# Loading the convolution's rows on GpSimd's queue, and a third landing buffer for the second weights

## The chip, the cores and the metric

The kernel runs on one core of a Trainium2 chip. The core has a matrix engine (TensorE, PE in the profile), three engines for elementwise work (VectorE is DVE, ScalarE is ACT, GpSimd is POOL) and SyncE (SP), which here only issues DMA transfers. PE's weight loads are shown apart as PEld. Every engine works through its own instructions in order; semaphores hold an instruction back until what it needs is there. A transfer is issued by an instruction on some engine's queue and moved by 16 DMA engines that all queues share.

The metric is the time of one execution in microseconds (us) on the device. The kernel before takes 1116.93 us, the median of three runs (1115.04 to 1117.27).

## What is computed

The input is one sequence of 2048 rows of 576 numbers. Its layer norm goes two ways, and both results are added to the input:

```
xn  = layernorm(x)
out = x + S4(xn) + silu(xn @ w1) @ w2          # w1: 576 x 4608, w2: 4608 x 576
S4:  A = A_re + i A_im,  dt = exp(log_dt)       # 576 channels, 128 states
     K[d,l] = Re sum_n C[d,n] dt[d] B[d,n] exp(dt[d] A[d,n] l)
     y[:,d] = causal convolution of xn[:,d] with K[d,:]  + xn[:,d] * Dskip[d]
```

The convolution is done by transforms: the kernel K and xn are brought to a spectrum, multiplied, and brought back.

## The kernel before, in words

**The feed-forward part** fills most of PE's time. The 2048 rows are taken in two halves, each half in two blocks of 512 rows, and the 4608 hidden columns in nine chunks of four tiles of 128 (t = 0 to 3). For a block and a chunk, `up` (lines 331 to 352) multiplies by the first weights into a PSUM tile `ph`, applies SiLU on ACT (`gf`), and splits the result into a high and a low part (`gh`, `gl`); `down` (354 to 376) multiplies by the second weights into `po` for four groups of 128 rows and two halves of 288 columns, and DVE adds that to the accumulators `acc`. Each product is made of three matmuls: high by high, high by low, low by high.

**Weights.** Each weight tile is loaded into a landing buffer and then split. For the second weights, `load_w2` (310 to 316) issues one transfer of 128 x 576 numbers into a buffer `w2r`, and `split_w2` (318 to 329) has ACT cast it to `w2h` (line 324) and DVE subtract to get `w2l` (326). A buffer is free again when its `w2l` is made. The buffers lie in the pool `wp`; for t = 2 and 3 of the very first chunk they lie in `pa`, and of the very last chunk in `yp`. All weight loads but the first are issued on SP's queue. The loads for a chunk are written into the steps of the chunk before it: t = 0 and 1 after the first block's second `up`, t = 2 in the second block's first step, t = 3 in its fifth. The loads for the last chunk are written earlier, all at the start of the last chunk but one.

**The spectral part** (`spectral`, from line 749) runs beside the second half of the feed-forward part. For 16 groups it loads spectra on POOL's queue, makes small matmuls (line 795), multiplies on DVE, goes back through matmuls into `pb` (line 846), and stores two tiles `yo` to DRAM (`d<-yo`, line 851). Its tiles lie in a pool `kl`.

**The tail** (`tail`, lines 894 to 914) begins when `kl` is released, because the pool `yp` takes that memory. It loads the stored accumulators of the first half (`r0`, line 900; the profile writes `r`), and the convolution's rows: `conv_load` (926 to 933) issues for one j two transfers of 64 x 4 x 288 numbers into a tile `ys`, of which there are eight. `add_conv` (935 to 954) makes sixteen small matmuls `py` for a pair of j, adds them with DVE (line 952), and calls `conv_load` for two further j. Finished rows are stored (line 194) on the queues of POOL, SP and ACT.

**Order.** The program text gives each piece of work a place, and side work is woven into the feed-forward steps by due times (`weave`, `side`). The order that each engine gets is then made by a planner, which runs the program on a modelled timeline (`schedule_with_timeline_sim=True`, line 1132) and puts each engine's ready instructions in the order of that timeline. A change of a queue or of a buffer count can therefore move instructions on every engine. The program gives the transfers of SP and ACT eight counters in turn and those of POOL eight others; an issue waits until the transfer that used its counter before has landed.

Of the kernel before, what the change touches and what calls it, by code (L numbers as in the profile page):

```python
# [11 lines left out]
F32 = mybir.dt.float32  # L12
# [7 lines left out]
P = 128  # L20
L = 2048
D = 576
# [21 lines left out]
def kernel(  # L44
# [22 lines left out]
    nc = tc.nc  # L67
# [38 lines left out]
    wp = ctx.enter_context(tc.tile_pool(name="wp", bufs=2))  # L106
# [160 lines left out]
    def ffn():  # L267
# [42 lines left out]
        def load_w2(half, c, t):  # L310

            first = half == 0 and c == 0
            last = half == 1 and c == NCH - 1
            r2 = (pa if first and t > 1 else yp if last and t > 1 else wp).tile([P, D], F32, tag="w2r", name="w2r", bufs=2)
            pins["load"] = nc.sync.dma_start(r2, w2v[:, c * FT + t, :]).ins  # L315
            R2[half, c, t] = r2

# [87 lines left out]
        for t in range(FT):  # L405
            load_w2(0, 0, t)
# [12 lines left out]
        for i, blk in enumerate(blocks):  # L419
# [4 lines left out]
            if half == 0 and c == NCH - 1:  # L424
                next_xt(b)

            after = {
                (0, "u0"): [(load_w1, 0)],
                (0, "u1"): [(split_w1, 0), (load_w2, 0), (load_w2, 1)],
                (0, "u2"): [(load_w1, 2)],  # L430
                (1, "u0"): [(split_w1, 2), (split_w2, 0), (load_w2, 2)],
                (1, "d3"): [(split_w2, 1), (load_w2, 3), (split_w2, 2)],
                (1, "u2"): [(split_w2, 3)],
# [460 lines left out]
    def tail():  # L894

        r0s = {}

        def load_r0(j):
            r0s[j] = yp.tile([P, 2, D], F32, tag="r0", name="r0", bufs=4)
            nc.sync.dma_start(r0s[j], dr0[j * P:(j + 2) * P, :].rearrange("(i p) d -> p i d", p=P))  # L900

        yield tail_at[0]
        with behind(pins["load"]):
            for j in (0, None, 2, None, None, None, None, None):
                conv_load()
                if j is not None:
                    load_r0(j)
        for j in range(0, 8, 2):
            if j == 2:
                load_r0(4)  # L910
                load_r0(6)
            yield tail_at[1 + j // 4] + j // 2 % 2 * tail_at[3]
            add_conv(j, (r0s[j][:, 0, :], r0s[j][:, 1, :]))
            store(r0s[j], j, (nc.gpsimd,))

    yss = {}
# [9 lines left out]
    def conv_load():  # L926

        j = next(order, None)
        if j is not None:
            yss[j] = yp.tile([P, 4, HD], F32, tag="ys", name="ys", bufs=8)  # L930
            for h in range(2):
                nc.sync.dma_start(yss[j][64 * h:64 * h + 64],  # L932
                                  d2[j * 256:(j + 1) * 256, h * HD:(h + 1) * HD].rearrange("(q r) d -> r q d", q=4))

    def add_conv(j, dsts):

        py = [pool.tile([P, 512], F32, tag=t, name="py") for pool, t in ((pss, "pss"),) * 3 + ((ps3, "ps3"),)]
        first = pins["pe"]
        for n in range(16):
            i, q1, q2, h = 1 - n // 8, n // 4 % 2, n // 2 % 2, 1 - n % 2  # L940
            o = 64 * q1 + 32 * q2
            rows = slice(64 * h, 64 * h + 64)
            with tc.high_priority() if n else nullcontext(), behind(first):
                mm = nc.tensor.matmul(py[2 * i + h][o:o + 32, :HD], s4[rows], yss[j + i][rows, 2 * q2 + q1],  # L944
                                      start=True, stop=True, tile_position=(64 * h, o), skip_group_check=True)
            if n == 0:
                first = mm.ins
        for i in range(2):
            del yss[j + i]
            for h in range(2):  # L950
                hs = slice(h * HD, (h + 1) * HD)
                nc.vector.tensor_add(dsts[i][:, hs], py[2 * i + h][:, :HD], dsts[i][:, hs])
        for _ in range(2):
            conv_load()
# [181 lines left out]
```

## Time and profile before

| | us |
|---|---|
| median of the runs | 1116.93 |
| the profiled execution | 1118.75 |
| its span, first to last instruction | 1116.9 |
| PE busy in the span | 1097.8 |
| PE waiting for `w2h` | 10.1 |
| landing time of a `w2r` load, median | 4.1 |
| landing time of a `ys` load, median | 7.1 |

The clock that PE was granted is 0.996 of full speed over the span. In a list of waits, a line names the engine and the work that waited, what it waited for, the total in us, how many times, and the longest. In a chain or a timeline, a line begins with its start and its duration in us. SPq is SP's queue issuing. In a transfer view, q1 is the queue of transfers that SP and ACT issue and q0 that of POOL, each with packets, MB and its share of the time of 16 DMA engines; an issue line ends with KB of one transfer and the median us from issue to landing.

### The profile page before, as it was taken

Reading aid. Unit: us, or ns where it says so; the run is one execution under the profiler, and the core shown is the slowest. Engines: PE = TensorE matmul, PEld = TensorE weight load, DVE = VectorE, ACT = ScalarE, POOL = GpSimd, SP = SyncE. Lnnn points to the kernel's source line nnn. Section 1 sums busy time; section 2 is a strip of 40 time slices with the busy share of each in tenths; the row PEclk is TensorE's granted clock in tenths of the full one; section 3 lists DMA queues with packets and bytes.
Section 4 is the critical chain, followed back from the end, with each engine's and each line's share of the span. In section 5 each row is a group of like instructions: output and inputs, shape, how many; then the busy total and the mean of one; then the engine's idle time right before and its main releaser. Section 6 shows DMA issues by size and latency. Waiting matters only on the chain. (4 is left out here: it accounts for less than half of the span.)

```text
span 1116.9 us, 23956 instructions
## 1 busy us (share of the span) xinstructions
PE 1097.8 (98%) x9807; PEld 962.2 (86%) x9807; DVE 892.1 (80%) x1431; ACT 660.7 (59%) x1030; POOL 141.8 (13%) x257
## 2 busy tenths in 40 slices
PE   9999999999999999999999999999999999996998
PEld 7989998899989888989999987878888888896886
DVE  7799899999999999999999637867786867442443
ACT  4665466676777676667777437576767576431220
POOL 1100000000000000011000033332332321000111
PEclk9999999999999999999999999999999999998999
DMA  9746512525252434275734185554555644294363
GB/s 254 203 122 166 148 45 60 129 72 130 72 130 72 109 99 93 73 185 178 187 108 97 42 215 164 172 158 143 178 178 159 191 136 121 82 239 127 92 164 86
DMA packets 174397, 150.22 MB, mean 135 GB/s; under 512 B 112544, under 2 KB 144048, under 8 KB 174160
## 3 DMA queue, kind: packets, MB, share of 16 engines
q1 hardware_dynamic: 156544, 93.77, 32.9%
q0 software_dynamic: 16992, 54.07, 15.4%
q8 instruction: 77, 1.26, 0.5%
q10 hardware_dynamic: 752, 0.85, 0.3%
q14 instruction: 32, 0.26, 0.1%
HBM read 104.13 MB, written 44.61 MB: 133 GB/s over the span
## 5 line engine op out<-in xcount | busy, mean ns | idle before, releaser
L367 PE MATMUL po<-w2h,gh 128*128 128x288 f32 x1152 | 338.6, 298 | 10.2 <-ACT w2h L324 10.1
L367 PE MATMUL po<-w2l,gh 128*128 128x288 f32 x1152 | 339.4, 296 | 0.4 <-DVE w2l L326 0.4
L367 PE MATMUL po<-w2h,gl 128*128 128x288 f32 x1152 | 337.0, 295 | 0.8 <-DVE gl L352 0.8
L367 PEld LDWEIGHTS po<-w2h,gh 128*128 128x128 f32 x1152 | 215.4, 188 | 26.9 <-ACT w2h L324 11.5
L367 PEld LDWEIGHTS po<-w2l,gh 128*128 128x128 f32 x1152 | 216.5, 188 | 7.8 <-issue 1.4
L367 PEld LDWEIGHTS po<-w2h,gl 128*128 128x128 f32 x1152 | 215.8, 188 | 3.3 <-issue 1.4
L349 ACT ACTIVATE gf<-ph 128x512 f32<-128x512 f32 (+1 forms) x146 | 85.7, 588 | 155.7 <-PE ph L343 145.8
L371 DVE TENSOR_TENSOR acc<-po,acc 128x288 f32<-128x288 f32 x288 | 125.9, 451 | 51.0 <-PE po L367 49.7
L341 PE MATMUL ph<-xh,w1h 128*128 128x512 f32 (+1 forms) x584 | 162.1, 390 | 0.0
L341 PE MATMUL ph<-xh,w1l 128*128 128x512 f32 (+1 forms) x584 | 159.7, 387 | 0.0
L341 PE MATMUL ph<-xl,w1h 128*128 128x512 f32 (+1 forms) x584 | 158.7, 387 | 0.0
L352 DVE TENSOR_TENSOR gl<-gf,gh 128x512 fp32r<-128x512 f32 (+1 forms) x148 | 98.6, 671 | 74.1 <-ACT gh L350 73.2
L341 PEld LDWEIGHTS ph<-xl,w1h 128*128 128x128 f32 x584 | 107.1, 188 | 21.5 <-issue 0.9
L341 PEld LDWEIGHTS ph<-xh,w1l 128*128 128x128 f32 x584 | 106.9, 188 | 21.0 <-issue 0.9
L341 PEld LDWEIGHTS ph<-xh,w1h 128*128 128x128 f32 x584 | 104.2, 188 | 18.1 <-issue 1.4
L350 ACT CAST gh<-gf 128x512 fp32r<-128x512 f32 (+1 forms) x148 | 89.3, 608 | 23.5 <-PE po L367 20.7
L174 POOL DMA_DIRECT2D d1u<-u x32 | 17.4, 545 | 463.5 <-ACT u L173 463.5
L326 DVE TENSOR_TENSOR w2l<-w2r,w2h 128x576 fp32r<-128x576 f32 x72 | 53.2, 750 | 18.7 <-ACT w2h L324 18.5
L324 ACT CAST w2h<-w2r 128x576 fp32r<-128x576 f32 x72 | 47.0, 672 | 31.6 <-DMA w2r<-in_B_w_dram 24.4
L663 ACT ACTIVATE c<-th,magic 128x1040 f32<-128x1040 f32 x36 | 42.1, 1168 | 37.1 <-DVE C L686 27.5
L832 ACT CAST yh<-y 128x576 fp32r<-128x576 f32 x32 | 21.6, 674 | 65.1 <-DVE y L829 53.2
L665 ACT ACTIVATE c<-th 128x1040 f32<-128x1040 f32 x36 | 38.7, 1075 | 32.8 <-DVE th L664 32.8
(196 smaller groups left out, 1779.4 us busy)
## 6 DMA issues: line engine op xcount, KB each, us to landing
w2r<-in_B_w_dram SPq DMA_DIRECT2D x72, 288.0 KB, 4.1
w1r<-in_B_w_dram SPq DMA_DIRECT2D x35, 512.0 KB, 4.0
d1u<-u POOLq DMA_DIRECT2D x32, 288.0 KB, 2.7
d1k<-stage SPq DMA_DIRECT2D x36, 256.0 KB, 4.7
u<-d1u POOLq DMA_DIRECT2D x16, 576.0 KB, 4.7
d<-yo POOLq DMA_DIRECT2D x32, 288.0 KB, 3.0
ys<-d SPq DMA_DIRECT2D x32, 288.0 KB, 7.1
xr<-dxn SPq DMA_DIRECT2D x16, 288.0 KB, 2.9
```

The lines of the kernel that those rows point to most:

```text
L174: nc.gpsimd.dma_start(d1u.rearrange("(p m j) d -> m j p d", m=2, j=NJ)[m, j], u1)
L324: pins["w2h"] = nc.scalar.copy(h2, r2).ins
L326: pins["w2l"] = nc.vector.tensor_sub(l2, r2, h2).ins
L341: nc.tensor.matmul(ph, w[:, kt, :], v[:, kt, a:e], start=n + kt == 0, stop=False)
L349: nc.scalar.activation(gf, ph, AF.Silu)
L350: pins["gh"] = nc.scalar.copy(gh, gf).ins
L352: pins["gl"] = nc.vector.tensor_sub(gl, gf, gh).ins
L367: pins["pe"] = nc.tensor.matmul(po[:, :HD], G[blk, t][g][:, js], W2[half, c, t][w][:, hs], start=n == 0, stop=n == 3 * FT - 1).ins
L371: nc.vector.tensor_add(acc[j][:, hs], po[:, :HD], acc[j][:, hs])
L663: nc.scalar.activation(c65, th, AF.Identity, bias=magic)
L665: nc.scalar.activation(c65, th, AF.Abs)
L832: nc.scalar.copy(yh, y)
```

## The change

Two lines change. In `load_w2` the landing buffer `w2r` has three instances instead of two where it lies in `wp`, which is everywhere but for t = 2 and 3 of the first and the last chunk. In `conv_load` the two transfers of a `ys` tile are issued on GpSimd's queue instead of SP's.

```diff
@@ load_w2
-            r2 = (pa if first and t > 1 else yp if last and t > 1 else wp).tile([P, D], F32, tag="w2r", name="w2r", bufs=2)
+            r2 = (pa if first and t > 1 else yp if last and t > 1 else wp).tile([P, D], F32, tag="w2r", name="w2r", bufs=2 if t > 1 and (first or last) else 3)
             pins["load"] = nc.sync.dma_start(r2, w2v[:, c * FT + t, :]).ins
             R2[half, c, t] = r2
@@ conv_load
             yss[j] = yp.tile([P, 4, HD], F32, tag="ys", name="ys", bufs=8)
             for h in range(2):
-                nc.sync.dma_start(yss[j][64 * h:64 * h + 64],
+                nc.gpsimd.dma_start(yss[j][64 * h:64 * h + 64],
                                   d2[j * 256:(j + 1) * 256, h * HD:(h + 1) * HD].rearrange("(q r) d -> r q d", q=4))
```

## The prediction

> **What bounds the kernel now.** I read the page's first part, then PE's waits, then the chain that ended last, and then SP's queue and the transfers where that chain stands still.
>
> ```profile
> span 1116.9 us, 23956 instructions
> PE 1097.8 (98%) x9807; PEld 962.2 (86%) x9807; DVE 892.1 (80%) x1431; ACT 660.7 (59%) x1030; POOL 141.8 (13%) x257
> ...
> PE po L367 <- ACT w2h L324: 10.1, 4, 8.6
> PE py L944 <- DVE r L952: 0.6, 1, 0.6
> PE po L367 <- DVE w2l L326: 0.4, 1, 0.4
> ```
>
> PE is busy for 98% of the span. The matmuls are the same in number and shape after the change, so only PE's idle time can be won: 1116.9 - 1097.8 = 19.1 us, part of it start and end. More than half of what can be won is one wait: of 10.1 us that PE waited for the high part of the second weights (w2h), 8.6 us are a single one. The chain shows where.
>
> ```profile
> 973.19 2.73 DMA d<-yo
> ...
> 978.45 7.02 DMA w2r<-in_B_w_dram
> ...
> 985.53 12.29 DMA w2r<-in_B_w_dram
> ...
> 998.45 10.58 DMA ys<-d
> ...
> 1009.10 9.89 DMA w2r<-in_B_w_dram
> ...
> 1019.01 0.68 ACT w2h L324
> 1019.68 0.04 issue
> 1019.73 1.09 PE po L367 x3
> ...
> 1025.21 2.72 PE ph L341 x12
> 1027.93 7.96 PE po L367 x60
> ```
>
> The last store of the spectral stage (d<-yo) lands at 975.92. From there the chain is transfers only, and PE comes back at 1019.73, when a tile of second weights that was issued at 1009.10 has landed (9.89 us) and been cast (0.68 us). It is the fourth tile (t=3) of the last chunk but one. SP's queue and the transfers show why it was so late:
>
> ```profile
> 976.19 0.38 SPq L288 DMA_DIRECT2D w1r<-in_B_w_dram  x1
> ...
> 977.82 1.06 SPq L315 DMA_DIRECT2D w2r<-in_B_w_dram  x2
> 978.92 2.55 SPq L932 DMA_DIRECT2D ys<-d  x2
> ...
> 984.17 0.54 SPq L288 DMA_DIRECT2D w1r<-in_B_w_dram  x1
> 985.53 0.35 SPq L315 DMA_DIRECT2D w2r<-in_B_w_dram  x1
> ...
> 992.72 13.40 SPq L932 DMA_DIRECT2D ys<-d  x10
> 1006.63 1.58 SPq L900 DMA_DIRECT2D r<-dr  x2
> 1009.10 11.73 SPq L315 DMA_DIRECT2D w2r<-in_B_w_dram  x3
> ...
> DMA packets 7330, 9.60 MB, mean 253 GB/s; under 512 B 480, under 2 KB 5741, under 8 KB 7328
> q1 hardware_dynamic: 7328, 9.57, 106.1%
> ys<-d SPq DMA_DIRECT2D x16, 288.0 KB, 10.4
> r<-dr SPq DMA_DIRECT2D x4, 576.0 KB, 10.2
> w2r<-in_B_w_dram SPq DMA_DIRECT2D x5, 288.0 KB, 9.4
> w1r<-in_B_w_dram SPq DMA_DIRECT2D x1, 512.0 KB, 11.7
> w1r<-in_B_w_dram SPq DMA_DIRECT2D x2, 64.0 KB, 11.0
> ```
>
> The last seven lines are the transfer view of 978 to 1016 us. All 16 DMA engines are full there (106.1% by this count) at 253 GB/s, all on SP's queue. The tile that PE waits for stands behind sixteen convolution loads of 288 KB, ten of which alone take 13.40 us to issue, because the built program lets an issue on SP wait for the transfer eight places before it.
>
> **The change, part by part.** *SP's queue loses 32 issues* (16 pairs). Of its work before the tile, 16 x 288 KB = 4.72 MB go. At 253 GB/s this is 18.7 us of transfer, twice the wait.
>
> *The third buffer.* Outside the first and last chunk a tile of second weights now waits for the split of the third tile before it, no longer of the second. In the built order t=2 stands right behind t=0 and t=1, and t=3 waits for the split of t=0 where it waited for that of t=1. The three smaller waits for w2h (10.1 - 8.6 = 1.5 us) and the one for its low part (0.4 us) are such late tiles, so I count 1.9 us gained. What stands behind these issues on SP goes out earlier with them.
>
> *POOL's queue gains 32 issues.*
>
> ```profile
> 971.34 0.30 PE L846 MATMUL pb<-yh,mm 128*128 128x288 f32 x1
> 972.65 1.08 POOL L851 DMA_DIRECT2D d<-yo  x2 [7.23 <-ACT yo L816]
> ...
> POOL out_dram L194 <- DVE r L952: 88.5, 4, 70.3
> ```
>
> At 1.08/2 = 0.54 us each that is 17.3 us of issuing, on a queue that idles up to 70.3 us after d<-yo: nothing on the path. In the built order twenty loads stand ahead of POOL's first output store; that store moves, the last ones do not, and the end is set by PE and the stores that follow it.
>
> *The planner orders every engine anew,* and this is where the change can lose what it gains. I counted in the two built orders, from the last matmul of the spectral stage (L846) to the first that needs the late tile. Before: 139 po and 92 ph. After: 111 po and 56 ph. With 7.96/60 = 0.133 and 2.72/12 = 0.227 us each that is 39.3 us before (971.34 + 39.3 = 1010.6, where PE did stop) and 27.4 us after: the spectral stage ends later in PE's order, and the tile is wanted sooner.
>
> SP cannot begin the load before the spectral stage's memory is free. That was 976.19 - 971.34 = 4.85 us after its last matmul, with nothing in that stretch that the change touches. In the new order SP then issues: w1r (640 KB), two w2r, all four r (576 KB each), 576 KB of the next w1r, and the tile. That is 640 + 576 + 2304 + 576 + 288 = 4384 KB = 4.49 MB that must land within 27.4 + 0.3 (PE drains what it has begun) - 4.85 - 0.72 (cast) = 22.1 us. About 1.5 us of it are latency: 288 KB alone took 2.73 us (d<-yo), 1.2 of them at 253 GB/s. There remain 20.6 us, so no wait needs 4.49/20.6 = 218 GB/s on SP's queue, while POOL's queue holds up to eight convolution loads at any time. How two full queues share the engines is the unknown. Two stretches of the spectral stage (656.5 to 661.5 and 680.5 to 683 us) have both queues full:
>
> ```profile
> DMA packets 1036, 1.51 MB, mean 301 GB/s; under 512 B 153, under 2 KB 786, under 8 KB 1035
> q1 hardware_dynamic: 820, 0.94, 66.7%
> q0 software_dynamic: 215, 0.56, 40.1%
> ...
> q1 hardware_dynamic: 255, 0.53, 71.1%
> q0 software_dynamic: 94, 0.22, 26.1%
> ```
>
> SP's queue (q1) got 0.94/5 = 188 and 0.53/2.5 = 212 GB/s, POOL's (q0) 112 and 88. The ends for the new wait: SP alone at 253 GB/s needs 17.7 us, no wait; half of 253 GB/s needs 35.6 us, a wait of 15.0 us. I take the two measured rates: 212 for the 3.24 MB of w2r and r (rows of 2304 bytes, as in the second stretch) and 188 for the 1.25 MB of w1r, 15.3 + 6.6 = 21.9 us, a wait of 1.3 us.
>
> The Trainium skill (DMA: Bandwidth & Descriptors, section Issuing engines are not separate DMA queues) says that transfers run on the same 16 engines whoever issues them, and that issuing from several engines saves only issue time. By this rule the 4.72 MB cost as much as before, and the move alone wins nothing; the two stretches agree that the queues share, and what I count on is the order in which bytes are served.
>
> *Other new waits of the new order* no row shows. Below they can be negative (the 0.6 us before py may go), above I allow 3 us, six of the mean small wait of 1.5/3 = 0.5 us. I take 1.0, two of them.
>
> **Sum.** The profiled execution took 1118.75 us (span 1116.9). -8.6 + 1.3 (the tile) - 1.9 (small waits) + 1.0 (new order) = -8.2, so 1110.5 in such an execution. The median of the runs, 1116.93, stands 1.82 below it: 1108.7.
>
> **The rivals.** *Even halves (slower).* If the engines give POOL's queue half their bytes, the tile lands 15.0 us late and the sum is -8.6 + 15.0 - 0.9 = +5.5: 1122.4. The point from which this decides is 4.49/(20.6 + 8.6 + 0.9) = 149 GB/s on SP's queue. Against it stand 188 and 212; for it, that neither stretch had the queues full for more than 5 us.
>
> *Turn by turn (no change).* If each queue sends one row in turn, SP's 2624 rows (1216 of 1024 bytes, 1408 of 2304) bring as many of 1152 from POOL, 3.02 MB: 7.51/0.253 = 29.7 us, a wait of 9.1 us, sum -0.4: 1116.5. Against it: 820 packets to 215 and 255 to 94, both stretches with q0 waiting.
>
> The Trainium skill (the same page, section Queues, rings and completion order) has each engine go round the queues it has work for, packet by packet, which would be this rival if a packet were one row. The counts do not agree with that reading.
>
> *Half the gain.* SP's queue reaches some 165 to 185 GB/s, or SP waits for its transfer eight places back while r is in flight: a wait of 3.7 to 6.6 us, 1111 to 1114.
>
> *The new order loses elsewhere (slower).* DVE at 80% is the next busiest; were its work put so that PE waits over 9 us in total, the time would pass 1117, up to 1120. Today PE waits 0.4 and 0.6 us for DVE in the rows above.
>
> *The convolution loads come too late from POOL.* After SP's bytes have landed at POOL's 88 GB/s, 1.9 of 4.72 MB are there by 22 us and the rest follows in 11 us. The new order has 204 po and 112 ph (52.5 us) between the last spectral matmul and the first py. Hidden; I give it nothing.
>
> **How the numbers follow.** Forecast 0.63 (1105 to 1111); half the gain 0.11; turn by turn 0.09; even halves 0.08; loss elsewhere 0.09. The range 1105.0 to 1117.5 leaves out the even halves, most of the loss elsewhere and a little below, where the last small waits would have to go as well. A change under 0.2% (2.2 us) is about what a measurement here cannot tell from none. Faster: 0.63 + 0.11 + 0.01; same: most of turn by turn, 0.08; slower: 0.08 + 0.09.
>
> **What would show it.** Right: the longest wait of PE for w2h under 3 us; t=3's load issued some 10 us after SP comes free and landing within 25; no ys on SP; POOL's wait for the first output store gone from 70 us. Wrong: a wait for w2h of 8 us or more at that place, with q0 at half of the transfers; PE waiting for py on a ys transfer; new waits for DVE of several us.

## The result and the profile after

The changed kernel takes 1130.14 us (1128.40 to 1131.98), the kernel before 1116.93 (1115.04 to 1117.27). The ratio is 1.0122, with a 95% interval of 1.0105 to 1.0139: 13 us slower, where 8 us faster was forecast.

The first part of the page and the waits of PE in the kernel after (a row of waits: us in total, times, longest):

```profile
span 1130.2 us, 23962 instructions
PE 1099.3 (97%) x9807; PEld 965.3 (85%) x9807; DVE 893.0 (79%) x1431; ACT 660.2 (58%) x1030; POOL 161.7 (14%) x289
...
PE po L367 <- ACT w2h L324: 17.3, 1, 17.3
PE po L367 <- DVE acc L371: 4.0, 3, 3.3
PE pt L134 <- DVE xn L212: 1.8, 3, 1.2
PE pz L978 <- DVE zero L973: 1.3, 1, 1.3
PE po L367 <- ACT gh L350: 0.8, 1, 0.8
PE py L944 <- DVE r L952: 0.6, 1, 0.6
```

The span grew by 13.3 us. Of that the waits for w2h are 17.3 - 10.1 = 7.2, the wait for `acc` 4.0, `gh` 0.8, `xn` 0.8 (1.8, before 1.0), and PE's busy time 1099.3 - 1097.8 = 1.5. Two small waits of before, for `w2l` (0.4) and `gl` (0.8), are gone. The sum is 13.1.

The three small waits for w2h are gone too. What is left is one wait of twice the old length, at the same tile, t=3 of the last chunk but one. The chain of work that ended last, and SP's queue, both in the kernel after (start, duration, what):

```profile
984.86 7.96 PE po L367 x60
...
993.73 1.59 PE po L367 x12
...
996.01 11.52 SPq L291
...
1007.63 17.98 DMA w2r<-in_B_w_dram
...
1025.64 0.68 ACT w2h L324
...
1026.36 5.46 PE po L367 x22
```

```profile
987.93 0.39 SPq L288 DMA_DIRECT2D w1r<-in_B_w_dram  x1
...
990.66 3.00 SPq L900 DMA_DIRECT2D r<-dr  x4
993.76 2.21 SPq L288 DMA_DIRECT2D w1r<-in_B_w_dram  x1
996.01 11.52 SPq L291 DMA_DIRECT2D w1r<-in_B_w_dram  x1
1007.63 2.56 SPq L315 DMA_DIRECT2D w2r<-in_B_w_dram  x1
```

SP came free at 987.93. No convolution load stands on its queue, and yet the tile was issued only at 1007.63, because the issue before it (L291) took 11.52 us. That was no wait for a transfer eight places back: the one that had used its counter landed at 994.29, before this issue began. What held it the trace does not show. It is not what made the tile late, since the four r loads issued ahead of it on the same queue landed only from 1008.0 to 1022.8. The tile landed at 1025.61, 37.7 us after SP came free. PE had stopped at 1026.36 - 17.3 = 1009.1. The transfer view of 996 to 1008 us says why SP's transfers crawled:

```profile
DMA packets 1042, 3.07 MB, mean 256 GB/s; under 512 B 135, under 2 KB 135, under 8 KB 1041
...
q0 software_dynamic: 519, 1.93, 66.1%
q1 hardware_dynamic: 522, 1.12, 38.0%
```

The two queues sent the same number of packets, 519 and 522. But POOL's (q0) carried 1.93/519 = 3.7 KB each and SP's (q1) 1.12/522 = 2.15 KB on average, so that SP's queue got 1.12/12 = 93 GB/s and POOL's 161. The sizes in the trace's list of packets that began in this stretch:

```
kernel after, 996 to 1008 us
POOL's queue (q0): 419 packets of 4608 bytes, 100 of 4 bytes
SP's queue   (q1): 487 packets of 2304 bytes,  35 of 4 bytes
kernel before, the same loads on SP's queue: packets of 1152 bytes
```

Four rows of 1152 bytes make 4608. The convolution loads went out as single rows on SP's queue, and four rows to a packet on POOL's. The packets of 4 bytes count in the averages above.

### The profile page after: what moved, and what is told of

It is laid out like the page before. It is cut to its first block, busy times and chain, and to the rows that moved or that the text cites. A ratio compares the mean times of both kernels' runs of the same rounds, so it can differ in the third digit from the quotient of the medians.

```text
span 1130.2 us, 23962 instructions
## 1 busy us (share of the span) xinstructions
PE 1099.3 (97%) x9807; PEld 965.3 (85%) x9807; DVE 893.0 (79%) x1431; ACT 660.2 (58%) x1030; POOL 161.7 (14%) x289
## 4 chain that ended last, share of the span: by engine, by line
PE 91%; DMA 4%; DVE 2%; SPq 1%; ACT 1%; issue 1%; POOL 0%; DVEq 0%; ACTq 0%; POOLq 0%
PE po L367 40%; PE ph L341 32%; PE kp L706 3%; PE ph L342 3%; PE ph L343 3%; PE pb L846 2%; PE z L721 2%; DMA w2r<-in_B_w_dram 2%; PE pk L795 2%; PE pu L795 1%; PE pu L171 1%; SPq L291 1%; PE py L944 1%; DMA acc<-in_A_u_dram 1%; PE pu L172 1%; DMA m<-in_cm_dram 1%
## 5 line engine op out<-in xcount | busy, mean ns | idle before, releaser
L367 PE MATMUL po<-w2h,gh 128*128 128x288 f32 x1152 | 342.1, 299 | 22.2 <-ACT w2h L324 17.3
```

The source lines that it names most:

```text
L367: pins["pe"] = nc.tensor.matmul(po[:, :HD], G[blk, t][g][:, js], W2[half, c, t][w][:, hs], start=n == 0, stop=n == 3 * FT - 1).ins
```

## The experiments

Three theories were told apart. T (turns): the queues take turns packet by packet, and POOL's large packets take the engines from SP's weights. P (plan): the new order of the engines costs the time. V (volume): what counts is only how many bytes are moved ahead of the tile, by whichever queue. The times of before in the three comparisons are 1117.45 (e1 to e4), 1117.21 (e5, e6) and 1117.62 us (e7).

**e1: the third buffer alone.** From the kernel after:

```diff
-                nc.gpsimd.dma_start(yss[j][64 * h:64 * h + 64],
+                nc.sync.dma_start(yss[j][64 * h:64 * h + 64],
```

> Only the third landing buffer; the convolution's rows stay on SP's queue. PE's order has the spectral stage's end and the late tile where the changed kernel has them. Theory T (turns: each DMA engine sends one packet from SP's queue and one from POOL's, and POOL's packets of the convolution's rows are about twice as large, so SP's queue gets some 95 GB/s while POOL's is full): with nothing on POOL's queue SP gets all of about 250 GB/s, 3.5 MB stand before and in the tile, it lands some 15.5 us after SP comes free and 20.5 are there, so PE's longest wait for w2h goes below 3 us and the time is 1108 to 1112. Rival P (plan: the third buffer's new order ends the spectral stage 6.6 us later and wants the tile 12 us sooner, and that is the loss): a wait of 8 to 17 us here too, 1117 or more. Rival V (volume: the engines are full with 9.3 MB whoever issues, and the tile comes when nearly all is through): a wait near 15 us, about 1128.

Measured: 1109.43 us (1107.54 to 1110.12), ratio 0.9928 (0.9912 to 0.9945). This kernel is faster than both. Its first part and PE's waits, its queue on SP around the tile, and its transfers of 996 to 1008 us:

```profile
span 1105.8 us, 23959 instructions
PE 1095.3 (99%) x9807; PEld 961.7 (87%) x9807; DVE 892.9 (81%) x1431; ACT 660.0 (60%) x1030; POOL 141.7 (13%) x257
...
PE po L367 <- DVE acc L371: 1.8, 2, 1.0
PE pt L134 <- DVE xn L212: 1.5, 2, 1.3
```

```profile
983.83 0.38 SPq L288 DMA_DIRECT2D w1r<-in_B_w_dram  x1
...
986.56 1.28 SPq L932 DMA_DIRECT2D ys<-d  x2
987.88 0.60 SPq L900 DMA_DIRECT2D r<-dr  x1
988.52 0.58 SPq L932 DMA_DIRECT2D ys<-d  x1
989.21 0.76 SPq L288 DMA_DIRECT2D w1r<-in_B_w_dram  x1
990.06 0.67 SPq L315 DMA_DIRECT2D w2r<-in_B_w_dram  x1
...
992.30 4.85 SPq L932 DMA_DIRECT2D ys<-d  x3
```

```profile
DMA packets 2444, 3.02 MB, mean 252 GB/s; under 512 B 158, under 2 KB 2059, under 8 KB 2443
...
q1 hardware_dynamic: 2443, 3.01, 107.9%
```

No wait for w2h is left at all. The third buffer lets the planner put t=3's load 6.2 us behind SP's first issue instead of 32.9 (before: 976.19 to 1009.10), with three convolution loads ahead of it in place of sixteen. The others stand behind it on the same queue, and SP's loads landed here in the order of their issue: the tile at 1000.4, 16.6 us after SP came free, and the next load of rows, issued at 992.30, at 1002.1. Only one of the four r loads stands ahead of the tile, where the kernel after has all four: 3.54 MB up to and with the tile in place of 4.49. At 253 GB/s that is 3.8 us of the 21.1 by which the tile lands sooner than in the kernel after (16.6 to 37.7). The engines are as full as in the kernel after (252 against 256 GB/s); only who is served differs. V falls: it expected a wait near 15 us. P falls: PE's order in e1 is that of the kernel after up to the tile's matmul. The spectral stage ends later in it as well than before (977.02 to 971.34), and that costs nothing.

**e2: the rows on POOL alone.** From the kernel before:

```diff
-                nc.sync.dma_start(yss[j][64 * h:64 * h + 64],
+                nc.gpsimd.dma_start(yss[j][64 * h:64 * h + 64],
```

> Only the move to POOL's queue; two landing buffers as before, and PE's order around the wait as before. T: SP's queue has 95 GB/s until POOL's 4.72 MB are through at 160 (29.5 us), then some 300. Tile t=2, which here stands behind the four accumulator loads again, is complete after 4.49 MB, some 36 us after SP comes free, and is wanted 28 us after: a wait of about 8 us, t=3 little more. About 1117, within 3 us of before. P: with the old order the move alone wins the 8.6 us: about 1108. V: like before, a wait of 8 to 9 us.

Measured: 1122.44 us (1121.44 to 1124.74), ratio 1.0045 (1.0027 to 1.0062). PE's and ACT's long waits, and the transfers of 996 to 1008 us:

```profile
PE ph L341 <- ACT gf L349: 13.7, 1, 13.7
...
ACT w2h L324 <- DMA w2r<-in_B_w_dram: 19.2, 1, 19.2
```

```profile
q0 software_dynamic: 514, 1.91, 65.0%
q1 hardware_dynamic: 517, 1.12, 38.4%
```

The same split, 514 to 517 packets. ACT stood 19.2 us in front of a cast for a tile of second weights, with `gf` behind it, and PE stopped for `gf`. Moving the rows costs 5.0 us by itself (1122.44 - 1117.45), and 20.7 us where the third buffer is there (1130.14 - 1109.43). P falls again, since PE's order is that of before up to the wait; T expected a wait of 8 us and V one of 8 to 9; both were some 5 us short, and this run does not tell them apart.

**e3: padded rows.** From the kernel after, to keep a partition's four rows apart in the tile:

```diff
-            yss[j] = yp.tile([P, 4, HD], F32, tag="ys", name="ys", bufs=8)
+            yss[j] = yp.tile([P, 4, HD + 8], F32, tag="ys", name="ys", bufs=8)[:, :, :HD]
```

> The changed kernel with each partition's four rows of ys 8 numbers apart in its tile, so that they are no longer one run of 4608 bytes on chip. T: if POOL's packets then hold one row of 1152 bytes, SP's queue gets about two thirds of the bytes (some 170 GB/s), the tile lands about 28 us after SP comes free instead of 37.7, and the wait falls from 17.3 to some 6 to 8 us: about 1120. If the packets stay as large, nothing changes (1130). P and V: 1130 in either case.

Measured: 1130.94 us (1129.93 to 1131.75), ratio 1.0123 (1.0108 to 1.0138), 505 packets to 504, POOL's again of 4608 bytes. The edit did not do what it was for: rows that lie apart are still put together. It says nothing on the size of packets, only that the split repeats.

**e4: the four r loads on POOL too.** From the kernel after:

```diff
-            nc.sync.dma_start(r0s[j], dr0[j * P:(j + 2) * P, :].rearrange("(i p) d -> p i d", p=P))
+            nc.gpsimd.dma_start(r0s[j], dr0[j * P:(j + 2) * P, :].rearrange("(i p) d -> p i d", p=P))
```

> The changed kernel with the four loads of stored accumulators (576 KB each) moved to POOL's queue as well; PE's order stays. T: SP's queue then has 2.13 MB up to the tile instead of 4.49; at 95 GB/s that is 22.4 us and 1.5 of latency against 20.5 that are there: a wait of 3 to 4 us, about 1116. V: all bytes are the same, a wait near 17 us, 1130. P: 1130.

Measured: 1118.50 us (1116.55 to 1121.72), ratio 1.0014 (1.0003 to 1.0026). The transfers of 996 to 1008 us:

```profile
q0 software_dynamic: 659, 2.50, 79.5%
q1 hardware_dynamic: 656, 0.68, 25.8%
```

SP's queue now holds first weights in packets of 1024 bytes (574 of its 656), and it still gets one packet for each of POOL's. Its rate falls from 93 to 0.68/12 = 57 GB/s with the size of its packets, as T's rule has it, though T's numbers had kept 95. The tile landed 25.6 us after SP came free, where T had said 23.9. The time falls nevertheless, because 2.36 MB less stand ahead of the tile on that queue: the longest wait is 6.4 us (for `gh`, behind a w2h that waits 11.7 for its tile). V expected no change, since all the bytes are still moved; it falls here.

**e5: each convolution load cut into four.** From the kernel after:

```diff
-                nc.gpsimd.dma_start(yss[j][64 * h:64 * h + 64],
-                                  d2[j * 256:(j + 1) * 256, h * HD:(h + 1) * HD].rearrange("(q r) d -> r q d", q=4))
+                for q in range(4):
+                    nc.gpsimd.dma_start(yss[j][64 * h:64 * h + 64, q, :],
+                                      d2[j * 256 + 64 * q:j * 256 + 64 * q + 64, h * HD:(h + 1) * HD])
```

> Each convolution load of 64 x 4 x 288 numbers is split into four of 64 x 288, still on POOL's queue, in the otherwise unchanged kernel after: the same bytes, at the same place, in packets that can be no longer than a row of 1152 bytes. T (the two queues take turns packet by packet, and POOL's packets of some 3.7 KB against SP's of 2.15 KB are what starves SP): the packets stay one to one, SP's queue gets 2.15/(2.15 + 1.15) = 0.65 of 253 GB/s, about 165; 4.49 MB then take 27 us and 1.5 of latency, the tile lands some 28.5 us after SP comes free where it was 37.7, PE's wait for w2h falls from 17.3 to about 8, the time to about 1121 (1118 to 1124). V (what counts is the bytes on the engines ahead of the tile, whichever way they are cut): wait 17, 1130. P (the new order of the engines costs the time): 1130 as well. A fourth outcome: POOL's packets do not get shorter, and nothing changes.

Measured: 1121.68 us (1120.59 to 1123.85), ratio 1.0038 (1.0024 to 1.0051). The transfers of 988 to 1008 us, and POOL's queue in that stretch:

```profile
DMA packets 3074, 5.81 MB, mean 290 GB/s; under 512 B 526, under 2 KB 1216, under 8 KB 3073
...
q1 hardware_dynamic: 2374, 4.18, 73.5%
q0 software_dynamic: 699, 1.61, 31.1%
```

```profile
991.57 0.52 POOL L933 DMA_DIRECT2D ys<-d  x1 [0.64 <-DMA ys<-d]
993.88 0.52 POOL L933 DMA_DIRECT2D ys<-d  x1 [1.79 <-DMA ys<-d]
995.48 3.72 POOL L933 DMA_DIRECT2D ys<-d  x7 [1.07 <-DMA ys<-d]
```

T's time was met (1121 expected) but for another reason than T gave. The packets stayed at 4608 bytes (323 of them from 990 to 1008 us), although a load now has one row of 1152 bytes for each partition: the rows of four partitions are put together. And the packets are not one to one, 2374 to 699. POOL now waits for its own earlier loads, of which eight can be in flight, and eight loads of 72 KB are a quarter of what eight of 288 KB were. That is not the whole of it: from 990.4 to 992.2 us POOL's queue sent 30 packets against 254 of SP's, with seven or eight of its loads issued and not yet landed. Why such small loads were served so seldom the trace does not show. SP's queue got 4.18/20 = 209 GB/s and the tile landed 25.5 us after SP came free (984.46 to 1009.91). V, which expected 1130, falls in so far as it put all of the rows' bytes ahead of the tile: when it landed, 1.96 of POOL's 4.72 MB had moved.

**e6: four tiles for the rows instead of eight.** From the kernel after:

```diff
-            yss[j] = yp.tile([P, 4, HD], F32, tag="ys", name="ys", bufs=8)
+            yss[j] = yp.tile([P, 4, HD], F32, tag="ys", name="ys", bufs=4)
```

> The kernel after with four instead of eight tiles for the convolution's rows, so that half of the bytes, 2.36 MB, go out on POOL's queue before the first convolution and the others wait for its end. T: POOL's queue takes 160 GB/s for 2.36/0.160 = 15 us, SP's 95 GB/s gives 1.4 MB in that time and 253 GB/s the other 3.1 MB in 12 us: the tile lands some 28.5 us after SP comes free (37.7 before), the wait for w2h falls from 17.3 to about 8, the time to about 1121, if no convolution then waits for its rows. V gives nearly the same, (4.49 + 2.36)/0.253 = 27 us. P: no change, 1130. A new wait of PE for py on a load of rows would show that four tiles are too few.

Measured: 1120.05 us (1118.71 to 1122.02), ratio 1.0024 (1.0010 to 1.0038). PE's longest wait, the transfers of 990 to 1000 us, and those of 1003 to 1009 us:

```profile
PE po L367 <- ACT w2h L324: 6.1, 1, 6.1
```

```profile
q0 software_dynamic: 426, 1.60, 65.7%
q1 hardware_dynamic: 449, 0.96, 38.4%
...
q1 hardware_dynamic: 1375, 2.28, 104.2%
q0 software_dynamic: 2, 0.00, 0.3%
```

While POOL's 2.36 MB last, SP's queue gets 96 GB/s; when they are through, 2.28/6 = 380. The tile landed 26.4 us after SP came free; T had said 28.5 and V 27, so this run does not tell those two apart. One wait of 0.9 us for a convolution load appears, so four tiles are nearly enough.

**e7: the rows on ACT's queue.** From the kernel after:

```diff
-                nc.gpsimd.dma_start(yss[j][64 * h:64 * h + 64],
+                nc.scalar.dma_start(yss[j][64 * h:64 * h + 64],
```

> The kernel after with the convolution's rows issued on ACT's queue instead of POOL's: another second queue beside SP's, whose packets should be single rows of 1152 bytes (on SP's queue in the kernel before these loads were such packets), where POOL's are of 4608 bytes. What is to be read is the stretch after SP comes free, in which both queues are full. T (packet by packet in turn, so that the share of the bytes follows from the packets' sizes): as many packets of the one queue as of the other, SP's of some 2.15 KB, so SP's queue gets 2.15/(2.15 + 1.15) = 65% of the bytes, about 165 GB/s of 253, where it got 95 beside POOL's. Rival K (a queue's kind decides, or the bytes are halved): SP's queue gets half of the bytes or less, 127 GB/s, and the packets are not one to one. The time says less: the loads' issues now stand between ACT's casts and hold them, since an issue waits for the transfer eight places before it; by T the tile lands some 28 us after SP comes free (37.7 beside POOL's), which gives about 1121, and ACT's own delays can add up to 10 us to that (1118 to 1131).

Measured: 1119.81 us (1119.42 to 1122.88), ratio 1.0028 (1.0018 to 1.0038). ACT's transfers are a queue of their own in the trace, q10; what is said further above, that q1 holds SP's and ACT's, is corrected by this. The transfers of 1015 to 1018 us, those of 999 to 1006 us, and those of 993 to 996 us:

```profile
q1 hardware_dynamic: 293, 0.60, 68.5%
q10 hardware_dynamic: 293, 0.32, 38.4%
...
q1 hardware_dynamic: 804, 1.21, 62.6%
q10 hardware_dynamic: 808, 0.88, 47.7%
...
q10 hardware_dynamic: 590, 0.63, 98.9%
q1 hardware_dynamic: 27, 0.06, 9.7%
```

In the first two stretches this is the test of packet size that e3 and e5 failed to be. The same rows go out in packets of 1152 bytes, the packets are again one to one (293 to 293, 804 to 808), and SP's queue gets 0.60/0.92 = 65% of the bytes while it sends rows of 2304, where beside POOL's it got 37%. With first weights mixed in (packets of 1024) it is 58%. K, by which SP's queue gets half or less whatever the packets' sizes, falls there. The third stretch does not fit: 27 packets stand against 590, although two r loads of SP's queue were on their way, and from 996 to 999 us it is the other way round, 448 to 83. So packet by packet is not the whole rule, and what decides in such stretches stays open. From 987 to 1018 us SP's queue got 56% of the bytes. The tile landed 18.5 us after SP came free, where T had said 28; only two of the four r loads stood ahead of it, and PE's order is another here too. The time gains less than the landing, because ACT's casts now wait behind the issues (the tile, landed at 1003.8, was cast at 1010.1):

```profile
ACT w2h L324 <- DMA ys<-d: 15.2, 1, 15.2
```

## Why the prediction was wrong

**What bounds the kernel: right.** The 8.6 us wait for t=3's tile could be won: e1 has no wait for w2h, and its span is 11.1 us shorter than before. (That wait is 45% of the 19.1 us of PE's idle time, not more than half, as I wrote.)

**The step that failed is the new wait for that tile, forecast at +1.3 us and measured at 17.3.** Its bytes were right (4.49 MB, the order of issues as counted), and so was the moment at which PE wants the tile: 27.8 us after the last spectral matmul (1009.1 - 981.22), forecast 27.4 and 0.3 of draining. What failed is the rate. I took 188 and 212 GB/s for SP's queue beside a full POOL queue, from two stretches of the spectral stage; it got 93. Counted from SP coming free, the tile landed 14.3 us later than the 23.4 (21.9 and 1.5) of the forecast. The stretches could not stand for the tail. POOL had loads on the way all through them, but by the order of issue some two thirds of what it moved there belonged to loads of 72 and 64 KB, and the counts, 820 to 215 and 255 to 94, look like those of e5 (2374 to 699), whose loads are of 72 KB and where SP's queue got 209 GB/s. Beside loads of 288 KB the packets were one to one within 6%, in the kernel after for 26 us (1197 to 1125 from 992 to 1018 us), and so they were in the stretches shown of e2, e3, e4 and e6. That the size of the loads is what makes the difference rests on e5 alone.

**A rival was set aside by a wrong size.** *Turn by turn* had the rule that the tail of the kernel after shows. Its size for POOL's packets, one row of 1152 bytes, stood against rows that I had quoted myself: 0.56 MB in 215 packets is 2.6 KB, and 0.22 in 94 is 2.3 KB. In the trace's list these are 108 packets of 4608 bytes, 15 of 4096 and 92 of 4, and 48 of 4608 and 46 of 4. With 3.7 KB by the count of packets, SP's share is 2.15/(2.15 + 3.7) = 37%, and all of POOL's 4.72 MB go before the tile: (4.49 + 4.72)/0.253 = 36.4 us and 1.5 of latency, 37.9, where 37.7 were measured. The Trainium skill (DMA: Bandwidth & Descriptors, section Queues, rings and completion order) says that an engine goes round the queues packet by packet, and that a packet can hold several descriptors, some 9 to 17. On the turns the trace agrees in the stretches named (519 to 522, 293 to 293), and not in e5 and in the rest of e7. On the size the trace has four rows in a packet on POOL's queue and one on SP's and ACT's. I had read "packet" as one row.

**Even halves named the outcome, not the cause.** It gave 37.1 us for the landing (35.6 and 1.5) and 1122.4. The landing came at 37.7, but as 37% of the bytes until POOL's were through and everything after that. The time came out 7.7 us above it.

**SP came free later than I took it to.** 987.93 - 981.22 = 6.7 us after the last spectral matmul, not 4.85. In e1 it is 6.8, in e2 4.9: the third buffer's order does it, which I had said touches nothing there. It took 1.9 us from the 22.1. With the 14.3 above and the 1.3 of the forecast that makes 17.5, where 17.3 were measured.

**The third buffer: right in kind, far too small.** The small waits for w2h and w2l went (1.9 us, as forecast). But I counted its main effect, the earlier place of t=3's load, only on the condition that the convolution loads leave SP's queue. e1 shows that it needs no such condition: the buffer alone gives -8.0 us by the timed runs (1109.43 - 1117.45). That is as much as was forecast for the whole change, by coincidence; the other half cost 20.7 us on top.

**The new order: +1.0 forecast.** Measured are 4.0 for `acc`, 0.8 for `gh` and 0.8 more for `xn`. One wait for `acc` of 3.3 us, at about 706 us, is in the kernel after and, with 3.3 and 3.2, in e3 and e4; it is 2.0 in e5, 1.4 in e7, and 1.0 in e1 and e6, though the lines follow one another on PE in the same order up to there. In its chain a load of `kw` takes 5.82 us in the kernel after and 4.26 in e1. What makes it longer stays open; it isn't the rows' queue alone, since e6 has that too.

**PE's busy time.** I held it fixed. It is 1095.3 us where no w2h wait is left (e1), 1097.8 with 10.1 us of it and 1099.3 with 17.3, at granted clocks of 0.999, 0.996 and 0.989. From 1000 to 1030 us, where the long waits lie, the clock is 1.00, 0.89 and 0.68. That a wait lowers the clock behind it is what these numbers suggest, and was not tried by itself; e4 has 1101.3 us with a longest wait of 6.4, so the length of the wait does not set it alone.

**The signs that I had listed** told it at once: q0 at 66% of the transfers, the wait for w2h over 8 us, a new wait for DVE. Right were: no convolution load on SP, and POOL's 70.3 us in front of its first output store gone (its three waits for `acc` at the stores add up to 18.2, the longest 10.5; it now waits 67.7 us in all in front of the convolution loads that follow a `py`).

## What to carry to other kernels

A second queue is not a waiting room: what was put on it here was served at once beside the queue that held the transfer PE waited for, in the kernel after packet for packet for 26 us, and the larger packets took the larger share. Where one load is urgent, put the bulk behind it on the same queue, as e1 does with a third landing buffer, or keep the bulk small in flight (e6). Before a share of two queues is taken from a stretch of the trace, look at the sizes of the packets on each, and make sure that the loads in it are as large as those it is to stand for.

## What the runs showed of the hardware that was not expected

The same transfer of 64 x 4 x 288 numbers went out in packets of 1152 bytes on SP's and ACT's queues and of 4608 on POOL's, and neither padding the tile's rows (e3) nor one row for each partition (e5) changed that. Full engines do not move the same everywhere: 252 GB/s in e1 while the rows went out one by one, 256 in the kernel after, 380 in e6 when SP's queue was alone with weights and accumulators. An issue can take long without its counter being the reason: 11.52 us in the kernel after, and 11.81 for the same line in e2, where the counter had been free since 982.94 and the issue began at 984.16. The Trainium skill (DMA: Bandwidth & Descriptors, section Issuing engines are not separate DMA queues) says that issuing from several engines saves only the time to issue. The engines are indeed shared, but in these runs the queue also decided who was served: the tile landed 37.7 us after SP came free with the rows on POOL's queue, and in e1, with the rows on SP's own, in time for PE not to wait.
